# Two tiles go through a layer in lockstep with two output banks each, weights of both layers of a pair are decoded together, and three convolutions run on PE at the start

## The chip, the cores and the metric

The kernel runs on one core of a Trainium2 chip. The metric is device time in microseconds, the median of several executions. The core has PE (TensorE, matrix products), DVE (VectorE), ACT (ScalarE), POOL (GpSimd) and SP (SyncE, which issues most DMAs). Each engine works its own queue in order, and engines wait for each other by semaphores.

## The reference

A causal convolution over the sequence, then two feed-forward layers. There are 16384 tokens of 192 numbers; each layer has 2048 hidden units.

```python
w = softmax(weight, axis=-1)                      # 8 heads x 7 taps
out[b, s, h] = sum_k w[h, k] * x[b, s + k - 6, h] # zeros before the start
x = out.reshape(16384, 192)
x = np.maximum(x @ w_in, 0.0) ** 2 @ w_out        # layer 1
h = x @ w_in2
x = np.maximum(0.01 * h, h) @ w_out2              # layer 2
```

The weights of both layers are float64 in HBM.

## The kernel before

**Tiles and products.** The 16384 tokens are cut into 32 tiles of 512. For accuracy each number is split into a high and a low part, and each product is made of three: high x high, low x high, high x low. The 192 rows of an operand are three blocks of 64. PE works as two halves of 64 rows (`halves`), and products come in pairs, one for each half, that run beside each other. `g1` makes two blocks of 128 hidden units (`h`, two PSUM banks): 18 products of 512 columns. `g2` adds them to the tile's output in four PSUM banks, 20 products for two hidden blocks. A step is one `g1` and one `g2` of the step before; a tile of a layer has 8 steps (`NP`), and the order of tiles is: four tiles of layer 1, two of layer 2, then one of each in turn. The program has 64 x 8 x 38 = 19,456 such products, and 56 more in the first steps that only keep PE busy (`keep_warm`).

**Output banks.** Each half of PE sums into banks of its own: `o[n][i]`, n for the first 128 and the last 64 output columns, i for the half. `evac` copies the four banks out (`take`, on ACT and DVE), adds the halves on DVE, lets GpSimd move 64 rows (L457) and adds again (L460).

**Between the products.** ACT makes `g` from `h` (`act`), ACT or DVE squares it in layer 1 (`square`), ACT rounds it to the high part `hi`, and DVE subtracts to get the low part `lo` (L416). The next `g2` needs `hi` and `lo`.

**Weights.** There are 16 pairs of hidden blocks, eight in each layer, numbered p. For each pair, `load_win` and `load_wout` bring 128 x 384 doubles each, and `decode` turns them into a high and a low part by six operations on DVE and two on ACT for each of the two. The first tile of layer 1 needs a new pair in every step, and so does the first tile of layer 2.

**Preparation.** `prep_tile` loads a tile of x, transposes it on DVE and makes the convolution there, 7 operations (taps) for each of two parts; `split_a` and `split_b` write its high part with ACT, `split_a_lo` and `split_b_lo` its low part with DVE, and then a DMA copies blocks from one half's partitions to the other's (`copy_half`, `x<-x`). One of the first tiles' convolutions is made on PE (`conv_pe`, 7 scaled diagonals).

**Order.** Within a step the order on each engine is that of the code. `pieces` adds single operations of preparation (`prep`), of evacuated tiles (`leave`) and of decoding (`dec`), at most so many a step and within a budget of DVE time. DMAs stand in SP's queue in the order of the program, but for a few on ACT's.

Of the kernel before, what the change touches and what calls it, by code (L numbers as in the profile page):

```python
# [20 lines left out]
WB = 3  # L21
STEP = 4100
DEBT = -4000
LEAD_I, LEAD_O = 2, 1
LEAD_X = 2.5
SPACE = 0.8
LEAVE = 5
WARM = 4
# [4 lines left out]
def conv_moe_moe2_kernel(  # L33
# [10 lines left out]

# [7 lines left out]
    NT = B * S // TT  # L61
    R = D - P
    HALO = 32
    HT = HALO + TT

    const = ctx.enter_context(tc.tile_pool(name="const", bufs=1))
    stage = ctx.enter_context(tc.tile_pool(name="stage", bufs=3))
    px = ctx.enter_context(tc.tile_pool(name="px", bufs=XB))
    p1 = ctx.enter_context(tc.tile_pool(name="p1", bufs=1))
    pz = ctx.enter_context(tc.tile_pool(name="pz", bufs=4))  # L70
    pg = ctx.enter_context(tc.tile_pool(name="pg", bufs=4))
    ph = ctx.enter_context(tc.tile_pool(name="ph", bufs=4))
# [3 lines left out]
    f32 = lambda ap: ap.bitcast(F32)  # L76
    halves = lambda i: slice(R * i, R * i + R)

    bias_e = const.tile([P, 1], F32, name="bias_e")
    nc.gpsimd.memset(bias_e, -896.0 * 2.0 ** 23)  # L80

    TURN = ((0, 1), (1, 0), (2, 2))
    W = {}
    for l in (1, 2):
        W[l] = dict(

            i=const.tile([P, NP, 3, 2, P], F32R, name=f"i{l}"),

            o=const.tile([P, NF, 2 * P + 2 * R], F32R, name=f"o{l}"),
        )
    w_in = {1: w_in1.bitcast(I32), 2: w_in2.bitcast(I32)}
    w_out = {1: w_out1.bitcast(I32), 2: w_out2.bitcast(I32)}
    NE = 3 * P

    scal = deque()

    def flush_scal():
        while scal:  # L100
            scal.popleft()()

    def decode(word, shape, outs):

        lo_w, hi_w = word[..., 0], word[..., 1]
        n = shape[1] * shape[2]
        view = lambda t: t[:, 0:n].rearrange("p (c d) -> p c d", d=shape[2])
        T = {}  # L110
        one, two = 70 + n * 52 // 100, 70 + n * 104 // 100

        def exponent():

            T["t"] = view(stage.tile([P, NE], I32, tag="t", name="t"))
            nc.vector.tensor_scalar(  # L116
                out=T["t"], in0=hi_w, scalar1=0x7FFFFE00, scalar2=None, op0=ALU.bitwise_and
            )

        def rebias():  # L120
            nc.scalar.activation(out=T["t"], in_=T["t"], func=ACTF.Relu, scale=8.0, bias=bias_e)

        def mantissa():
            T["m"] = view(stage.tile([P, NE], I32, tag="m", name="m"))
            nc.vector.tensor_scalar(out=T["m"], in0=hi_w, scalar1=0x1FF, scalar2=None, op0=ALU.bitwise_and)  # L125

# [247 lines left out]
    def keep_warm(u, n):  # L374

        if not ready:
            ready.append(a_bank())
# [415 lines left out]
```

## Time and profile before

| | |
|---|---|
| median of 3 runs | 2216.11 us (2214.8 to 2217.06) |
| span of the profiled execution | 2215.3 us |
| PE, DVE, ACT, POOL busy | 97%, 66%, 65%, 4% of the span |
| PE busy in the first of 40 slices | 70% |
| mean granted clock of PE | 0.993 |

The profiled execution's own time is not told apart from its span; the span lies within the times of the three runs. Busy shares of PE overlap, since products are pipelined: how far PE is from its best pace is read from the number of products in a stretch, not from its busy time.

### The profile page before, as it was taken

The numbers are of one execution on the slowest core, as the hardware profiler recorded it, in microseconds if no ns is written. First come the engines' busy times: TensorE is split into PE (matmuls) and PEld (weight loads), VectorE is DVE, ScalarE is ACT, GpSimd is POOL, SyncE is SP. The second block draws the span as 40 slices with busy tenths as digits, with TensorE's granted clock in tenths as the row PEclk, the third lists the DMA queues.
The fourth block names the chain that finished last, engine by engine and source line by source line (L and its number), as shares of the span: only waits on it lengthen the run. The fifth ranks groups of instructions, "written<-read, shape, count | busy, mean of one in ns | idle before, by whom it ended". The sixth has DMA issues, their size and how long they took to land.

```text
span 2215.3 us, 46852 instructions
## 1 busy us (share of the span) xinstructions
PE 2155.8 (97%) x19554; PEld 1810.3 (82%) x19554; DVE 1469.1 (66%) x2345; ACT 1445.9 (65%) x2681; POOL 80.1 (4%) x143
## 2 busy tenths in 40 slices
PE   7988999999999999999999999999999999999998
PEld 3866888888888888888888888888888888888887
DVE  7757855766756676665766666676665767666554
ACT  4868656666666666666666666666666666666664
POOL 0000000000000000000000000000000000000000
PEclk8999999999999999999999999999999999999999
DMA  5223211121212112122221212112121221211111
GB/s 131 75 65 84 43 31 38 35 37 29 44 36 46 37 26 48 25 44 40 39 39 20 44 35 46 37 27 46 26 44 39 41 42 17 47 29 38 37 23 15
DMA packets 227256, 91.09 MB, mean 41 GB/s; under 512 B 204516, under 2 KB 214756, under 8 KB 227044
## 3 DMA queue, kind: packets, MB, share of 16 engines
q1 hardware_dynamic: 224772, 86.74, 20.0%
q8 instruction: 152, 2.49, 0.5%
q10 hardware_dynamic: 2272, 1.38, 0.3%
q14 instruction: 60, 0.49, 0.1%
HBM read 25.17 MB, written 12.58 MB: 17 GB/s over the span
## 4 chain that ended last, share of the span: by engine, by line
PE 85%; ACT 6%; DVE 5%; issue 2%; DMA 1%; SPq 0%; ACTq 0%; POOL 0%; DVEq 0%; POOLq 0%
PE o L362 45%; PE h L362 40%; ACT hi L412 2%; ACT g L399 1%; ACT g L408 1%; DVE lo L416 1%; DVE g L406 1%; DVE t L135 1%; ACT x L349 1%; DVE m L128 1%; DMA w<-in_moe_w_in_dram 0%; DVE t L116 0%; ACT x L337 0%; PE conv L303 0%; DVE m L125 0%
## 5 line engine op out<-in xcount | busy, mean ns | idle before, releaser
L362 PE MATMUL h<-x,i 64*128 64x512 f32 x9272 | 1103.1, 377 | 13.5 <-DVE i L150 7.7
L362 PEld LDWEIGHTS h<-x,i 64*128 64x128 f32 x9272 | 893.4, 187 | 139.2 <-DVE i L150 8.0
L416 DVE TENSOR_TENSOR lo<-g,hi 128x512 fp32r<-128x512 f32 x1024 | 693.2, 695 | 293.7 <-ACT hi L412 275.3
L362 PE MATMUL o<-hi,o 64*128 64x512 f32 x6144 | 873.0, 377 | 3.2 <-ACT hi L412 2.9
L362 PEld LDWEIGHTS o<-hi,o 64*128 64x128 f32 x6144 | 600.3, 186 | 93.5 <-ACT hi L412 5.5
L412 ACT CAST hi<-g 128x512 fp32r<-128x512 f32 x1024 | 605.9, 620 | 96.3 <-DVE g L406 95.4
L362 PE MATMUL o<-lo,o 64*128 64x512 f32 (+1 forms) x4096 | 641.3, 378 | 27.9 <-DVE lo L416 27.4
L401 ACT ACTIVATE g<-h 128x512 f32<-128x512 f32 x512 | 277.8, 594 | 382.2 <-PE h L362 382.2
L362 PEld LDWEIGHTS o<-lo,o 64*128 64x128 f32 (+1 forms) x4096 | 342.4, 159 | 144.9 <-DVE lo L416 52.9
L399 ACT ACTIVATE g<-h 128x512 f32<-128x512 f32 x512 | 301.0, 588 | 230.4 <-PE h L362 230.1
L406 DVE TENSOR_TENSOR g<-g 128x512 f32<-128x512 f32 x224 | 161.0, 719 | 144.5 <-ACT g L399 144.1
L408 ACT ACTIVATE g<-g 128x512 f32<-128x512 f32 x288 | 182.8, 635 | 8.2
L292 DVE SCALAR_TENSOR_TENSOR acc_a<-xT_a,taps,acc_a 128x512 f32<-128x512 f32 x180 | 134.0, 745 | 2.7
L457 POOL COPY z<-z 64x512 f32<-64x512 f32 x64 | 56.0, 875 | 1660.8 <-DVE z L455 1636.2
L455 DVE TENSOR_TENSOR z<-z 128x512 f32<-128x512 f32 x128 | 83.2, 680 | 0.0
L452 DVE COPY z<-o 128x512 f32<-128x512 f32 x128 | 82.0, 682 | 1.0 <-PE o L362 1.0
L340 DVE TENSOR_TENSOR x<-z,x 128x512 fp32r<-128x512 f32 x32 | 22.1, 691 | 87.4 <-ACT x L337 87.4
L340 DVE TENSOR_TENSOR x<-acc_a,x 128x512 fp32r<-128x512 f32 x30 | 21.1, 704 | 81.7 <-ACT x L337 81.7
L292 DVE SCALAR_TENSOR_TENSOR acc_b<-xT_b,taps,acc_b 128x512 f32<-128x512 f32 x96 | 71.9, 749 | 1.8
L452 ACT COPY z<-o 128x512 f32<-128x512 f32 x128 | 69.0, 596 | 1.8 <-PE o L362 1.8
L353 DVE TENSOR_TENSOR x<-z,x 64x512 fp32r<-64x512 f32 x32 | 21.8, 683 | 71.0 <-ACT x L349 71.0
L460 DVE TENSOR_TENSOR z<-z 64x512 f32<-64x512 f32 x64 | 43.2, 676 | 2.3 <-POOL z L457 2.3
(67 smaller groups left out, 399.9 us busy)
## 6 DMA issues: line engine op xcount, KB each, us to landing
x<-x SPq DMA_DIRECT2D x189, 256.0 KB
raw_a<-in_x_dram SPq DMA_DIRECT2D x128, 64.0 KB
out_dram<-y_a SPq DMA_DIRECT2D x126, 64.0 KB
w<-in_moe_w_out_dram SPq DMA_DIRECT2D x16, 384.0 KB
raw_b<-in_x_dram SPq DMA_DIRECT2D x64, 64.0 KB
out_dram<-y_b SPq DMA_DIRECT2D x63, 64.0 KB
w<-in_moe_w_in_dram SPq DMA_DIRECT2D x15, 192.0 KB
w<-in_moe_w_in_dram SPq DMA_DIRECT2D x45, 64.0 KB
```

The costliest lines, as they stand in the source:

```text
L292: nc.vector.scalar_tensor_tensor(out=acc[0], in0=src, scalar=w, in1=acc[0], op0=ALU.mult, op1=ALU.add)
L340: nc.vector.tensor_sub(out=operand_view(X[u][:, 0, 1, :]), in0=taken(u, src), in1=operand_view(f32(X[u][:, 0, 0, :])))
L362: nc.tensor.matmul(out=o.rearrange("p (b a) -> p b a", a=2), lhsT=w, rhs=z.rearrange("p (a b) -> p b a", a=2), start=begin, stop=end_,)
L399: nc.scalar.activation(out=g, in_=hps.pop((u, f)), func=ACTF.Relu)
L401: nc.scalar.activation(out=g, in_=hps.pop((u, f)), func=ACTF.Prelu, alpha=0.01)
L406: nc.vector.tensor_mul(out=g, in0=g, in1=g)
L408: nc.scalar.activation(out=g, in_=g, func=ACTF.Square)
L412: nc.scalar.copy(out=a, in_=gsp[u, f])
L416: nc.vector.tensor_sub(out=b, in0=gsp.pop((u, f)), in1=f32(hi[u, f]))
L452: (nc.vector.tensor_copy if i else nc.scalar.copy)(out=z[n, i], in_=o[n][i])
L455: nc.vector.tensor_add(out=z[n, 0], in0=z[n, 0], in1=z[n, 1])
L457: nc.gpsimd.tensor_copy(out=z[1, 1][0:R], in_=z[1, 0][R:2 * R])
```

## The change

**Lockstep.** A phase now is a layer for two tiles (`u = (l, q)`, tiles 2q and 2q + 1). A step is one `g1` of one of them, pair p for tile i, so that a weight pair serves two steps. 512 steps of 18 + 20 products. `g2(u, f)` adds one hidden block f of both tiles, two steps after the `g1` (`LAG`). The order is two phases of layer 1, two of layer 2, and so on.

**Banks.** Each tile has two banks, `m` for 128 columns and `r` for 64. In a first part of `g2`, half 0 of PE writes tile 0's bank `m` and half 1 tile 1's; in a second part they change over. An instruction of GpSimd waits for the last product of the first part, and the first product of the second part waits for GpSimd. Two groups of `g1` (`AHEAD`, two pairs) stand between the parts. In the next step the second part's assignment is kept for the first.

**Evacuation.** Per two tiles: ACT and DVE copy one bank `m` each, ACT copies 64 rows of each bank `r`, and DVE adds 64 rows of each. Nothing of it is on GpSimd, and the small halo copies of the convolution move from GpSimd to DVE.

**Decoding.** The input and output weights of a pair are decoded as 768 columns, except the first pair (two parts of 384). The last three operations are made in two pieces of 640 and 128 columns, since the results lie in two tensors.

**Start.** The convolutions of the first two tiles, three of 7 taps, are on PE; 14 diagonals are made, 10 of them on DVE and 4 on ACT. Part of x is issued from ACT's queue. Weights are loaded up to three pairs ahead in two buffers and in the space of one later tile. The 56 products of `keep_warm` are gone.

The core of the diff:

```diff
+    def decode(l, p, t, a, b):
+
+        lo_w, hi_w = t[:, a:b, 0], t[:, a:b, 1]
+        n = b - a
+        one, two = 160 + n * 52 // 100, 170 + n * 104 // 100
+        e = min(b, NM)
+        parts = [(lambda z: z[:, 0:e - a], W[l][:, p, 0, a:e], W[l][:, p, 1, a:e])]
+        if b == NW:
+            r = WR[l][:, p]
+            parts.append((lambda z: z[:, NM - a:n].rearrange("p (c d) -> p c d", d=R), r[:, :, 0:R], r[:, :, R:2 * R]))
...
-    def g2(u, p):
-        if p == 0:
...
-        for f in (2 * p, 2 * p + 1):
-            a, b = hi.pop((u, f)), lo.pop((u, f))
-            first, last = f == 0, f == NF - 1
-
-            seq = [(o1, m, a), (o1, ml, a), (o2, r, a), (o2, rh, b), (o1, m, b)]
...
-            for n, (o, c, z) in enumerate(seq):
-                begin = first and id(o) not in begun
...
-                for i in range(2):
-                    v = halves(i)
-                    product(o[i][0:rows], w[v, f, c], z[v], begin, end_)
...
+    def g2(u, f):
...
+        l, q = u
+        if f == 0:
+            ops[u] = {(i, n): ps_o.tile([P, TT], F32, tag=f"o{i}{n}", name=f"o{i}{n}") for i in range(2) for n in "mr"}
+        o = ops[u]
+        a = [hi.pop(((l, 2 * q + i), f)) for i in range(2)]
+        b = [lo.pop(((l, 2 * q + i), f)) for i in range(2)]
+        main = [("m", "m", a), ("m", "ml", a), ("m", "m", b)]
+        rest = [("r", "r", a), ("r", "rh", b)]
+        if f == NF - 1:
+            rest = rest[::-1]
+        for part in range(2):
+            side = part ^ (f % 2)
+            for j, (n, c, z) in enumerate(main + rest):
+                begin = f == 0 and part == 0 and j in (0, 3)
+                end_ = f == NF - 1 and part == 1 and j in (2, 4)
+                for half in range(2):
+                    i = (side ^ half) if n == "m" else 1 - (side ^ half)
+                    v = halves(half)
+                    rows = R if c == "rh" else P
+                    ins = product(o[i, n][0:rows], weights_out(l, v, f, c), z[i][v], begin, end_).ins
+                    if part == 0 and j == 4 and half == 1:
+                        done = nc.gpsimd.nop(nofuse=True).ins
+                        tc.add_manual_dep(done, ins.name, in_turn, reason="halves take turns on a bank")
+                    if part == 1 and j == 0 and half == 0:
+                        tc.add_manual_dep(ins, done.name, in_turn, reason="halves take turns on a bank")
+            yield
...
-        def take(n, i):
-            z[n, i] = pz.tile([P, HT], F32, tag="z", name="z")[:, 0:TT]
-            (nc.vector.tensor_copy if i else nc.scalar.copy)(out=z[n, i], in_=o[n][i])
-
-        def add(n):
-            nc.vector.tensor_add(out=z[n, 0], in0=z[n, 0], in1=z[n, 1])
-            if n == 1:
-                nc.gpsimd.tensor_copy(out=z[1, 1][0:R], in_=z[1, 0][R:2 * R])
-
-        def add_r():
-            nc.vector.tensor_add(out=z[1, 0][0:R], in0=z[1, 0][0:R], in1=z[1, 1][0:R])
-
-        now = [lambda n=n, i=i: take(n, i) for n in range(2) for i in range(2)]
-        adds = [(690, lambda: add(1)), (690, lambda: add(0)), (690, add_r)]
...
+        def take(i):
+            z[i] = new(i)
+            (nc.vector.tensor_copy if i else nc.scalar.copy)(out=z[i], in_=o[i, "m"])
+
+        def shift(i):
+            if i == 0:
+                z["s"], z["r"] = f32(stage.tile([P, NW], I32, tag="m", name="zs")[:, 0:TT]), new("r")
+            nc.scalar.copy(out=z["s"][halves(i)], in_=o[i, "r"][halves(1 - i)])
+
+        def add(i):
+            v = halves(i)
+            nc.vector.tensor_add(out=z["r"][v], in0=o[i, "r"][v], in1=z["s"][v])
+
+        now = [(0, lambda: take(0)), (690, lambda: take(1))]
+        for i in range(2):
+            now += [(0, lambda i=i: shift(i)), (690, lambda i=i: add(i))]
...
-    for s, z in enumerate(steps):
-        first_use.setdefault(("w", z[0][0], z[1]), s)
-        first_use.setdefault(z[0], s)
-
-
-    todo = []
-    for l in (1, 2):
-        for p in range(NP):
-            s = first_use["w", l, p]
-            todo += [(s - LEAD_I, load_win, l, p), (s + 1 - LEAD_O, load_wout, l, p)]
...
-        load_taps()
+        nc.vector.memset(warm_e, 0.0)
+        nc.scalar.activation(out=warm_e, in_=warm_e, func=ACTF.Exp)
+        nc.sync.dma_start(out=w_taps, in_=weight)
...
+        nc.gpsimd.memset(idle, 0.0)
+        make_heads()
+        load_x("b", 0, nc.scalar)
+        load(0)
...
         make_taps()
-        keep_warm_early(3)
-        refill()
-        decode_ahead(1000)
+        keep_warm_early(2)
+        load(1)
+        load(2)
         transpose("a", 0)
         acc0 = conv_pe(xT["a"])
-        decode_ahead(1400)
         transpose("b", 0)
-        accb, pieces = conv("b", 0)
+        for k in range(K):
+            spread_v(1, k)
+        accb = conv_pe(xT["b"], 1)
+        decode_ahead(9)
+        transpose_second()
+        acc1 = conv_pe(second)
         split_a((1, 0), acc0)
...
+        decode_ahead(2)
+        split_a_lo((1, 0), acc0)
+        load(3)
+        decode_ahead(8)
+        split_b((1, 0), accb)
+        split_b((1, 1), accb)
+        decode_ahead(3)
+        split_b_lo((1, 0), accb)
+        split_b_lo((1, 1), accb)
+        decode_ahead(8)
+        split_a((1, 1), acc1)
+        split_a_lo((1, 1), acc1)
+        load_x("b", 2)
+        load_x("a", 2)
...
+        prep_next = 1
+        late = []
+        going = begin_g1(0)
+        for s in range(NS):
+            u, p, i = steps[s]
+            l, q = u
+            t = (l, 2 * q + i)
+            j = 2 * p + i
+            run(going)
+            follows = begin_g1(s + 1) if s + 1 < NS else None
+            leaving = []
+            if s >= LAG:
+                u2, p2, i2 = steps[s - LAG]
+                f = 2 * p2 + i2
+                if s == NS - 2:
+                    run(follows)
+                elif f == 0:
+                    run(follows, GAP)
+                z = g2(u2, f)
+                run(z, 1)
+                if follows:
+                    run(follows, AHEAD)
+                run(z)
+                if f == NF - 1:
+                    leaving, then = evac(u2)
```

**PE, a steady step.** Before, within the second hidden block of one step and the first of the next; `o_1534` and `o_1535` are the two halves' banks of one output, and names in brackets are the semaphores waited for.

```order
L362 MATMUL o_1536<-hi,o_85 128x512
L362 MATMUL o_1537<-hi,o_85 128x512
L362 MATMUL o_1536<-lo,o_85 64x512 [waits DVE_49]
L362 MATMUL o_1537<-lo,o_85 64x512
L362 MATMUL o_1534<-lo,o_85 128x512
L362 MATMUL o_1535<-lo,o_85 128x512
L362 MATMUL o_1534<-hi,o_85 128x512 [waits Activation_49]
L362 MATMUL o_1535<-hi,o_85 128x512
```

Now, from the end of a first part to the beginning of the second; `o0m` and `o0r` are tile 0's banks, `o1m` and `o1r` tile 1's.

```order
L356 MATMUL o0r<-hi,wr_90 128x512
L356 MATMUL o1r<-hi,wr_90 128x512
L356 MATMUL o0r<-lo,wr_90 64x512
L356 MATMUL o1r<-lo,wr_90 64x512
L356 MATMUL h<-x,w_88 128x512 [waits PE_49,Activation_49]
L356 MATMUL h<-x,w_88 128x512 [waits Activation_49]
L356 MATMUL h<-x,w_88 128x512 x2
L356 MATMUL o0m<-hi,w_88 128x512 [waits Pool_sequencer_49]
L356 MATMUL o1m<-hi,w_88 128x512
```

Four products of `g1` have moved between the two parts, and the second part's first product waits for GpSimd's sequencer.

**DVE while weights are decoded.** Before, between two steps' `lo` in the first tile (`t` and `m` are scratch, `w` the loaded doubles).

```order
L416 TENSOR_TENSOR lo<-g,hi 128x512 x2
L116 TENSOR_SCALAR t<-w 128x384
L125 TENSOR_SCALAR m<-w 128x384
L128 SCALAR_TENSOR_TENSOR m<-w,m 128x384
L135 SCALAR_TENSOR_TENSOR t<-w,t 128x384
L145 TENSOR_SCALAR t<-t 128x384
L150 SCALAR_TENSOR_TENSOR o_85<-m,t 128x2x128
L150 SCALAR_TENSOR_TENSOR o_85<-m,t 128x2x64
L116 TENSOR_SCALAR t<-w 128x384
L125 TENSOR_SCALAR m<-w 128x384
L128 SCALAR_TENSOR_TENSOR m<-w,m 128x384
L135 SCALAR_TENSOR_TENSOR t<-w,t 128x384
```

Now, in one of the first 16 steps.

```order
L401 TENSOR_TENSOR lo<-g,hi 128x512 x2
L141 TENSOR_SCALAR t<-w 128x768
L132 TENSOR_SCALAR m<-wide 128x768
L135 SCALAR_TENSOR_TENSOR wide<-wide,m 128x768
L286 SCALAR_TENSOR_TENSOR acc_b<-xT_b,taps,acc_b 128x512 x2
L401 TENSOR_TENSOR lo<-g,hi 128x512 x2
L145 SCALAR_TENSOR_TENSOR t<-w,t 128x640
L145 SCALAR_TENSOR_TENSOR t<-w,t 128x128
L151 TENSOR_SCALAR t<-t 128x640
L151 TENSOR_SCALAR t<-t 128x128
L156 SCALAR_TENSOR_TENSOR w_88<-w,t 128x640
L156 SCALAR_TENSOR_TENSOR wr_90<-w,t 128x2x64
```

Between two steps' `lo` stands half of a pair's decoding with taps of the next tiles' convolution, where both halves of a pair stood.

## Rows read from the trace of the kernel before

**Rows 1.** span and mean granted clock of the core
```profile
core 0: 2215.3 us, clock 0.993
```

**Rows 2.** timeline, a steady step: start, length (us), engine, line, operation, names
```profile
999.76 2.11 PE L362 MATMUL h<-x,i 64*128 64x512 f32 x18
...
1001.90 0.60 ACT L399 ACTIVATE g<-h 128x512 f32<-128x512 f32 x1 [0.98 <-PE h L362]
...
1003.86 2.11 PE L362 MATMUL h<-x,i 64*128 64x512 f32 x18
```

**Rows 3.** L362's products by stretch: busy us (x number), PEclk, DMA share, GB/s
```profile
0.00:60.00 60.00, 21.21 (x150) 17.00 (x151) 0.86 0.51 121
...
60.00:250.00 190.00, 165.57 (x1402) 135.38 (x1401) 0.97 0.27 70
...
250.00:2205.00 1955.00, 1944.56 (x17948) 1647.42 (x17946) 1.00 0.19 36
...
2205.00:2215.40 10.40, 2.15 (x20) 1.43 (x18) 0.74 0.25 38
```

**Rows 4.** waits of weight loads, 60 to 250: us, times, longest
```profile
PEld o L362 <- DVE lo L416: 25.9, 29, 3.1
```

**Rows 5.** timeline, PE after a wait near 117 us
```profile
118.57 3.31 PE L362 MATMUL h<-x,i 64*128 64x512 f32 x18
```

**Rows 6.** groups by line and shape: busy us, mean ns, idle before
```profile
L362 PEld LDWEIGHTS h<-x,i 64*128 64x128 f32 x9272 | 893.4, 187 | 139.2 <-DVE i L150 8.0 <-DMA x<-x 3.6 <-ACT x L349 2.1
...
L416 DVE TENSOR_TENSOR lo<-g,hi 128x512 fp32r<-128x512 f32 x1024 | 693.2, 695 | 293.7 <-ACT hi L412 275.3
...
L399 ACT ACTIVATE g<-h 128x512 f32<-128x512 f32 x512 | 301.0, 588 | 230.4 <-PE h L362 230.1
...
L408 ACT ACTIVATE g<-g 128x512 f32<-128x512 f32 x288 | 182.8, 635 | 8.2
...
L292 DVE SCALAR_TENSOR_TENSOR acc_a<-xT_a,taps,acc_a 128x512 f32<-128x512 f32 x180 | 134.0, 745 | 2.7
...
L128 DVE SCALAR_TENSOR_TENSOR m<-w,m 128x384 f32<-128x384 uint32 x32 | 19.9, 621 | 1.0
...
L121 ACT ACTIVATE t<-t,bias_e 128x384 int32<-128x384 int32 x32 | 19.7, 616 | 14.5 <-DVE t L116 13.1 <-DVE m L125 1.3
...
L150 DVE SCALAR_TENSOR_TENSOR i<-m,t 128x384 fp32r<-128x384 f32 x16 | 8.9, 558 | 0.5
...
L150 DVE SCALAR_TENSOR_TENSOR o<-m,t 128x128 fp32r<-128x128 f32 x16 | 4.5, 284 | 0.0
```

**Rows 7.** timeline, the start: a load, its use, a convolution
```profile
7.83 1.87 SPq L172 DMA_DIRECT2D w<-in_moe_w_in_dram  x3
...
9.18 3.60 PE L303 MATMUL conv<-xT_a,spare_acc_a 128*128 128x512 f32 x8
...
11.43 0.36 DVE L116 TENSOR_SCALAR t<-w 128x384 int32<-128x384 int32 x1 [2.79 <-DMA w<-in_moe_w_in_dram]
```

**Rows 8.** timeline and line L457: hand-overs from engine to engine
```profile
33.22 0.68 DVE L416 TENSOR_TENSOR lo<-g,hi 128x512 fp32r<-128x512 f32 x1
...
33.96 0.48 PE L362 MATMUL o<-lo,o 64*128 64x512 f32 x2 [1.38 <-DVE lo L416]
...
34.28 0.38 PE L362 MATMUL o<-hi,o 64*128 64x512 f32 x2
...
42.36 0.70 DVE L276 STREAM_TRANSPOSE xT_second<-raw_a 128x512 f32<-128x512 f32 x1
...
43.19 0.19 POOL L277 COPY xT_a<-xT_second 128x6 f32<-128x6 f32 x1 [28.86 <-DVE xT_second L276]
...
L457 POOLq EVENT_SEMAPHORE  x64: 17/17/43, 114.1 to 2210.0; - x64
```

**Rows 9.** timeline, the end: last products, last store
```profile
2206.77 0.38 PE L362 MATMUL o<-hi,o 64*128 64x512 f32 x2
...
2212.21 0.32 SPq L483 DMA_DIRECT2D out_dram<-y_b  x1
```

More of the change, by code (lines that the diff above doesn't have):

```diff
@@ L93, in conv_moe_moe2_kernel @@
[L93 to L109, printed above, removed]
-        T = {}
[L111 to L121, printed above, removed]
+    warm_e = const.tile([P, 1], F32, name="warm_e")
@@ new lines, in decode, with room, operand @@
+        last = [(c, lambda fn=fn: each(fn)) for c, fn in ((two, sign), (one, power), (two, low_))]
+        return [(one, mantissa), (two, rest)], [(one, exponent)], last
+    X, order, split = {}, [], set()
+    g1_left = {(l, t): NP for l in (1, 2) for t in range(NT)}
+    def room(u):
+        return u in X or len(order) < XB or g1_left[order[len(order) - XB]] == 0
+    def operand(u):
+        if u not in X:
+            assert room(u)
+            X[u] = px.tile([P, 3, 2, TT], F32R, tag="x", name="x")
+            order.append(u)
+        return X[u]
@@ new lines, in conv_moe_moe2_kernel, with load @@
+        loads = [(l, p) for l in (1, 2) for p in range(NP)]
+        words, since = {}, {}
+        SIDE = {2: 0, 3: 1, 5: 0}
+        AFTER = {0: 4, 1: 6, 2: 5, 4: 7, 6: 8}
+        def load(n):
+            if n >= len(loads):
+                return
+            l, p = loads[n]
+            since[n] = now[0]
+            if n in SIDE:
+                t = wide[:, SIDE[n] * 2 * NW:(SIDE[n] + 1) * 2 * NW].rearrange("p (c w) -> p c w", w=2)
+            else:
+                t = stage.tile([P, NW, 2], I32, tag="w", name="w", bufs=2)
+            load_w(l, p, t)
+            words[n] = t
@@ L554, in decode_one @@
+        budget = [0]
         def decode_one():
[L555 removed]
+            cost, fn = dec.popleft()[1:3]
             fn()
[L557 to L569 removed]
@@ L570, in conv_moe_moe2_kernel, with decode_ahead @@
-        bank = ps_o.tile([P, TT], F32, tag="o11", name="idle_o")
+            budget[0] -= cost
+            return cost
+        def decode_ahead(n):
+            for _ in range(n):
+                decode_one()
+        bank = ps_o.tile([P, TT], F32, tag="o1r", name="idle_o")
         def keep_warm_early(n):
@@ L766 @@
+        high(*late[0])
+        low(*late.pop())
+        while leave:
+            leave.popleft()[2]()
+        for f in range(NF - LAG, NF):
+            run(g2(steps[-1][0], f))
+        at_once, then = evac(steps[-1][0])
+        for c, fn in at_once:
+            fn()
+        for z in then:
+            z[1]()
 _INS = ["x", "weight", "moe_w_in", "moe_w_out", "moe2_w_in", "moe2_w_out"]
```

615 lines of the change are left out of this document (275 added, 340 removed).

## The prediction

> **What bounds the kernel now.** I began with the span [rows 1] and a step of the steady middle, in order of time. There a step of 38 products (19 pairs, one for each half of the array) starts every 1003.86 - 999.76 = 4.10 us [rows 2], 0.2158 us a pair or 0.1079 us a product, with no idle mark on PE. That is the fastest pace in the trace, and the change leaves the number of products at 19,456, so 19,456 x 0.1079 = 2099.3 us is a floor for both kernels. Whatever can be won is what the span has above it: 116 us.
>
> Where these lie shows in the table of stretches, which counts products [rows 3]; a stretch less 0.1079 us for each product is its loss. To 60 us: 94 useful products (150 less the 56 that only keep PE warm, which the reader counts in the code), loss 49.9. From 60 to 250 us: 38.7. From 250 to 2205 us: 18.4. After that: 8.2. So three quarters of the loss lies in the first 250 us, while weights are decoded; the long middle loses under 1%. The waits of 60 to 250 us name the reason: PE's weight loads stood 25.9 us for `lo`, which DVE makes [rows 4]. DVE decodes there, in its one queue, between the `lo`. [...]
>
> **The change part by part.** The sum is made against the profiled execution: span 2215.3 us, with some 0.8 us around it to the median of 2216.1.
>
> *Lockstep and the first 16 steps.* Before, one tile asks for a new weight pair in every step of 4.1 us. A pair costs DVE, from [rows 6] (the operations not listed taken as their likes of the same size): six bit operations of 0.401, four two-input ones of 0.621, then 0.558, 0.284 and, by the line between these two, 0.42 for the 256 columns between, together 6.15 us. With two `lo` of 0.695 that is 7.5 us of DVE in a step of 4.1: PE must wait. After, a pair serves two steps. Joint decoding makes it, by the line through 128 columns at 0.284 and 384 at 0.558 (1.07 ns a column and 0.147 us fixed), about 5.6 us; if nothing were fixed, 6.15 again. So DVE has, for the 16 steps of the first two tiles: 32 `lo`, 22.2; what is then left to decode (four pairs and half of one), 25.4; the preparation of the next two tiles (21 taps of 0.745, three transposes and four subtractions near 0.70), 20.5. Sum 68.1 us. ACT has 32 times an activation, a square and a cast, 0.588 + 0.635 + near 0.59, 58.0 us; its share of decoding, two casts of 768 columns a pair or about 1.8 us, 8.1; four casts of an operand, 2.5. Sum 68.6. PE needs 65.6. So DVE and ACT both run 3 us over, and each in its one queue waits for the other. I take 10 us lost in this phase: 3 of excess and 7 of such waits. Bounds: 3, and the 25.9 of [rows 4].
>
> *The second 16 steps.* DVE: 22.2 of `lo`, 16 squares near 0.70 (11.2), two thirds of eight pairs (29.9), evacuation and operands 4.8: 68.1 against 65.6. I take 3 us (0 to 10). Later phases have less than a step's 4.1 us on either engine.
>
> *The start.* Three convolutions on PE are 42 products of about 0.43 us [rows 7]: 18 us from about 8 us on, so 26 us; before, one was there and DVE did the others. But PE's first steps wait for more. The second tile's copies are issued behind its subtraction, and DVE's queue up to there holds the first three pairs (6.15 for the one in two parts, 2 x 5.6), three operations of the fourth (2.4), seven scaled diagonals of about 0.25, two transposes, four subtractions (2.8): 25.7 us from about 7.9, so 33.6 us if DVE never waits. (The small halo copies that move from GpSimd to DVE, 0.19 each by [rows 8], and the four issues of x that move from SP to ACT are inside these roundings: DVE has to wait for the diagonals, and ACT for the first weights, anyway; without that cover they cost 2 us.) Two copies at about 0.6 us on SP, then 1.7 to land (the load issued by 9.70 was used at 11.43 [rows 7]): 37 us. The first two tiles' first steps, 18 pairs or 3.9 us, are done at about 37.7, loss 33.8. PE stood before that, so I add 3 us at half clock, as in [rows 5]. 37 us. Below, nothing that DVE must do goes away: 31. Above, DVE waits for weights, whose loads stand in SP's one queue with the copies: 47.
>
> Together the decode stage loses 37 + 10 + 3 = 50 us instead of 88.6.
>
> *The token.* Each step of the second layer's products now ends its first part with a hand-over: its last product tells GpSimd, GpSimd tells PE, and the second part's first product waits, with everything behind it in PE's queue. Two pairs of `h` lie between. 512 of them. From the start of that last pair, T: the first reader of a pair started at 1001.90, and that pair at 999.76 + 8 x 0.2158 = 1001.49, so 0.41 [rows 2]. GpSimd's own wait instruction takes 0.017, a copy there began 0.13 after its producer (43.19 against 43.06). From DVE's end at 33.90 to PE's weight load at 33.96 it is 0.06 [rows 8]. So the load may start between T + 0.49 and T + 0.60. It has to start by T + 0.647 - 0.107 = T + 0.54: after a wait the next pair came 0.32 later, 0.107 more than usual, so that much of a load shows. The token is thus between 0.05 early (nothing) and 0.06 late (509 x 0.06 = 31 us). I take nothing, since the instruction is the same as the 0.017 one and no copy follows it. Three tokens at the end have no cover: 3 x (0.49 + 0.107 - 0.216), 1.1 us.
>
> [...]
>
> *Lag and evacuation.* g2 runs two steps behind g1, so `lo` has a whole step more. Before, four half sums are copied and added, three additions a tile and one copy on GpSimd; after, DVE and ACT do three small operations each for two tiles. None of that was on the path except at changes of tile. New is that all four banks are claimed together: from the end of one pair of tiles to the next lie 12 pairs, 2.6 us, plus three main pairs before the shifted bank is written. In layer 1 ACT's queue there is an activation, two casts, a square and an activation (3.0 us) and then three copies near 0.6, and DVE's last addition 0.7: 5.5 us after g1 against 5.6 needed. An operand's cast ahead of them makes it 0.6 late. I take 0.25 for 30 changes, 7.5 us, and 4.5 us for steps in which preparation fills DVE: 12 instead of 18.4. Bounds: 0, and 30 x 0.7 + 9 = 30.
>
> *The end.* Before, from the last products to the last store's issue 5.8 us [rows 9], 8.2 in all. After, one copy, two additions, three transposes on DVE and twelve stores on two queues, about 0.5 us longer, and 1.1 for tokens: 10 (9 to 13).
>
> **Sum.** 2099.3 + 50 + 0 + 12 + 10 = 2171.3, with 0.8 around it 2172, and about 1 for the products at the edges, which the table counts twice: 2173 us, 43 below the median.
>
> **The rivals.** *The decode stage gains half.* DVE and ACT stay the bound and wait for each other as now: 25.9 instead of 10, and 47 for the start: 2173 + 26 = 2199. For it speaks that both are over 100% for 16 steps; against it, that weights are decoded up to three pairs ahead and `lo` has a step of slack. Chance 0.18.
>
> *The banks become the wait.* 30 changes at 0.7 and full preparation steps: 2173 + 18 = 2191. For: ACT's queue order. Against: the second layer's queue has no square. Chance 0.10.
>
> *The token is late, and the kernel slower.* If GpSimd answers like its copies (T + 0.60) and the waiting load must be whole, 0.187 as in the group of weight loads [rows 6], it must start by T + 0.46, is 0.14 late, and 509 x 0.14 = 71 us make 2244. The gain is gone from 43 / 509 = 0.085 us late on. For: PE's queue lets nothing pass a waiting product. Against: the 0.017 row, and the 0.107 that a load cost after a wait. Chance 0.10; in between (0.02 to 0.08 late, 2183 to 2214), 0.06.
>
> That the change doesn't do what it says would mean PE at the old loss to 250 us, 2212: chance 0.03. The forecast has the rest, 0.53.
>
> **How the numbers follow.** The forecast's own range is 2158 to 2190: 6 less at the start, 7 in the first phase, 3 after it; 10 and 7 more. With the other cases in up to 2214, and only the slow token (0.10) and the best of the forecast (0.06) out, 2155 to 2214. A measurement of this kernel can tell about 0.2% (4 us) from no change. Faster holds all but the slow token, what lies over 2212, and half of the 0.03: 0.86. Same 0.04, slower 0.10.
>
> **What would show it.** Right: a step of 4.10 us across a token, with no idle mark on the product behind it; PE at full count from about 40 us, and 300 to 2150 us within 12 us of the floor; about 50 us lost to 250 us; decode groups of 768 columns near 1.1 us for two-input operations. Wrong: a gap before every second part (GpSimd as releaser, some 509 times); PE waiting for `lo` past 100 us in many steps; waits for ACT's copies of `o` once in 16 steps; copies `x<-x` that land after 40 us because SP issues weight loads ahead of them.

## The result and the profile after

The changed kernel takes 2192.07 us (median of four runs, 2190.58 to 2193.05), the kernel before 2216.59 us beside it: a ratio of 0.989, 95% interval 0.9876 to 0.9904. That is 24.5 us faster, where the forecast had 43. 2192 is 19 us above the forecast of 2173 and 2 us above the forecast's own range of 2158 to 2190; it lies inside the wider range with the rivals, 2155 to 2214.

The profiled execution's span and clock, which answer to [rows 1]:

```profile
core 0: 2190.3 us, clock 0.995
```

The page's line of busy times, and its chain of the work that ended last, by engine:

```profile
PE 2150.3 (98%) x19510; PEld 2016.6 (92%) x19510; DVE 1339.2 (61%) x2127; ACT 1417.5 (65%) x2601; POOL 3.4 (0%) x19
...
PE 90%; DVE 5%; ACT 3%; DMA 1%; issue 1%; SPq 1%; DVEq 0%; POOL 0%; POOLq 0%
```

The products of L356 by stretch, which answer to [rows 3] (busy us and number on PE, the same for weight loads, granted clock, DMA share, GB/s); the stretch that [rows 3] ends at 250 us is cut at 120 us, where the first two tiles are through layer 1:

```profile
0.00:60.00 60.00, 24.37 (x180) 20.56 (x182) 0.94 0.68 145
60.00:120.00 60.00, 49.46 (x413) 40.17 (x410) 0.94 0.29 71
120.00:250.00 130.00, 124.49 (x1113) 113.64 (x1115) 1.00 0.23 64
250.00:2150.00 1900.00, 1896.80 (x17503) 1805.92 (x17501) 1.00 0.20 36
2150.00:2190.30 40.30, 28.65 (x256) 24.78 (x252) 0.88 0.17 23
```

A stretch less 0.1079 us for each product is its loss, as in the prediction: 40.6, 15.4, 9.9, 11.4 and 12.7 us. The first three are the decode stage: 65.9 us, where the forecast had 50 and the kernel before 88.6. The last two, some 24 us, were forecast at 22. (The products at the edges, counted in two stretches, are the 1 us that the sum lacks to the span less the floor of 2099.3.) So 16 of the 19 us lie in the decode stage, and most of what follows is about those first 250 us.

The waits of PE's weight loads over the whole span show the same (us in all, times, longest); of 24.9 us for `lo`, 21.9 lie before 250 us, against 25.9 in [rows 4]:

```profile
PEld o1m L356 <- DVE lo L401: 24.9, 25, 5.6
...
PEld o1m L356 <- ACT hi L397: 8.9, 10, 2.1
PEld h L356 <- DMA x<-x: 7.7, 3, 5.2
...
PEld o1m L356 <- POOLq L429: 1.1, 2, 0.6
PEld o0m L356 <- POOLq L429: 1.1, 2, 0.6
```

The last two lines are the token: four waits in all, those at the end that nothing covers.

Three moments of the timeline before 120 us name most of them. Operands: DVE ends the second tile's subtraction at 34.05 us (the forecast said 33.6), SP issues its two copies at once, and PE's weight load that waits for the second of them starts at 40.71 us:

```profile
33.36 0.69 DVE L320 TENSOR_TENSOR x<-conv,x 128x512 fp32r<-128x512 f32 x1 [1.61 <-ACT x L317]
...
34.21 1.15 SPq L302 DMA_DIRECT2D x<-x  x2
...
38.40 0.69 DVE L401 TENSOR_TENSOR lo<-g,hi 128x512 fp32r<-128x512 f32 x1 [4.35 <-ACT hi L397]
...
40.71 5.22 PEld L356 LDWEIGHTS h<-x,w 64*128 64x128 f32 x33 [0.98 <-DMA x<-x]
```

So 6.5 us pass from issue to use, and DVE stands idle for 4.35 us meanwhile. Then, from 55 to 90 us, PE waits once in every 5.2 to 5.7 us for `lo`, each time some 1.5 us:

```profile
59.05 0.18 PEld L356 LDWEIGHTS o1m<-lo,w 64*128 64x128 f32 x1 [1.46 <-DVE lo L401]
...
64.72 0.18 PEld L356 LDWEIGHTS o1m<-lo,w 64*128 64x128 f32 x1 [1.49 <-DVE lo L401]
...
69.91 0.18 PEld L356 LDWEIGHTS o1m<-lo,w 64*128 64x128 f32 x1 [1.23 <-DVE lo L401]
```

At 95.8 us DVE's queue stops for weights. The first operation on the ninth pair (`m<-w`, L132) waits for its load, and the eighth pair's last operations (L145 to L156), an operand, a transpose and two `lo` stand behind it:

```profile
98.28 0.68 DVE L132 TENSOR_SCALAR m<-w 128x768 int32<-128x768 int32 x1 [2.49 <-DMA w<-in_moe_w_out_dram]
98.99 1.23 DVE L135 SCALAR_TENSOR_TENSOR w<-w,m 128x768 f32<-128x768 uint32 x1
100.11 1.04 DVE L145 SCALAR_TENSOR_TENSOR t<-w,t 128x640 int32<-128x640 int32 x2
...
104.65 1.25 DVE L401 TENSOR_TENSOR lo<-g,hi 128x512 fp32r<-128x512 f32 x2
```

### The profile page after: what moved, and what is told of

It reads as the page before. It is cut to its first block, busy times and chain, and to the rows that moved or that the text cites. A ratio compares the mean times of both kernels' runs of the same rounds, so it can differ in the third digit from the quotient of the medians.

```text
span 2190.3 us, 46974 instructions
## 1 busy us (share of the span) xinstructions
PE 2150.3 (98%) x19510; PEld 2016.6 (92%) x19510; DVE 1339.2 (61%) x2127; ACT 1417.5 (65%) x2601; POOL 3.4 (0%) x19
## 4 chain that ended last, share of the span: by engine, by line
PE 90%; DVE 5%; ACT 3%; DMA 1%; issue 1%; SPq 1%; DVEq 0%; POOL 0%; POOLq 0%
PE h L356 42%; PE o1m L356 14%; PE o0m L356 14%; PE o0r L356 10%; PE o1r L356 9%; ACT hi L397 1%; DVE lo L401 1%; DVE acc_a L286 1%; DMA w<-in_moe_w_out_dram 1%; ACT g L393 0%; DVE t L145 0%; ACT g L384 0%; ACT w L148 0%; DVE g L391 0%; PE idle_o L590 0%
## 5 line engine op out<-in xcount | busy, mean ns | idle before, releaser
L356 PE MATMUL h<-x,w 64*128 64x512 f32 x9216 | 1203.3, 377 | 6.8 <-DMA x<-x 6.5
L356 PEld LDWEIGHTS h<-x,w 64*128 64x128 f32 x9216 | 1003.1, 187 | 59.4 <-DMA x<-x 7.7
L356 PE MATMUL o1m<-hi,w 64*128 64x512 f32 x2048 | 610.5, 378 | 5.3 <-ACT hi L397 5.1
L356 PE MATMUL o0m<-hi,w 64*128 64x512 f32 x2048 | 609.4, 377 | 0.2
L356 PE MATMUL o1m<-lo,w 64*128 64x512 f32 x1024 | 388.5, 379 | 14.9 <-DVE lo L401 14.7
L356 PEld LDWEIGHTS o1m<-hi,w 64*128 64x128 f32 x2048 | 360.9, 185 | 30.5 <-ACT hi L397 8.9
L356 PE MATMUL o1r<-hi,wr 64*128 64x512 f32 x1024 | 388.4, 379 | 0.0
L356 PE MATMUL o0r<-hi,wr 64*128 64x512 f32 x1024 | 386.9, 378 | 0.0
L356 PE MATMUL o0m<-lo,w 64*128 64x512 f32 x1024 | 386.5, 377 | 0.0
L356 PE MATMUL o0r<-lo,wr 64*64 64x512 f32 x1024 | 385.3, 376 | 0.0
L356 PE MATMUL o1r<-lo,wr 64*64 64x512 f32 x1024 | 385.3, 376 | 0.0
L356 PEld LDWEIGHTS o0m<-hi,w 64*128 64x128 f32 x2048 | 362.4, 185 | 21.0 <-POOLq L429 1.1
L356 PEld LDWEIGHTS o1m<-lo,w 64*128 64x128 f32 x1024 | 190.7, 186 | 25.4 <-DVE lo L401 24.9
L356 PEld LDWEIGHTS o1r<-hi,wr 64*128 64x128 f32 x1024 | 190.7, 186 | 6.5 <-issue 4.8
L356 PEld LDWEIGHTS o0r<-hi,wr 64*128 64x128 f32 x1024 | 190.8, 186 | 1.6
L356 PEld LDWEIGHTS o0m<-lo,w 64*128 64x128 f32 x1024 | 190.7, 186 | 0.4
```

The lines of the kernel that those rows point to most:

```text
L356: return nc.tensor.matmul(out=o.rearrange("p (b a) -> p b a", a=2), lhsT=w, rhs=z.rearrange("p (a b) -> p b a", a=2), start=begin, stop=end_,)
```

## The experiments

All start from the changed kernel. Losses are worked out as above, for the stretches to 60, 60 to 120 and 120 to 250 us: 40.6, 15.4 and 9.9 in the changed kernel. In e3, e7, e10, e13 and e14 a few lines are added that finish a half decoded pair before an evacuation, since both use one buffer; they are meant to move nothing by themselves, which no run shows alone. The kernel before was timed again beside each group of runs, and its medians there run from 2214.4 to 2216.6 us; so a difference of 2 us between runs of two groups is not clear of noise, and the traces carry the argument.

**The eighth pair ahead of the ninth (e1).**

```diff
-                stage_(j + 1, 0)
-                stage_(j, 2)
+                if parts[j][0] == 7:
+                    stage_(j, 2)
+                    stage_(j + 1, 0)
+                else:
+                    stage_(j + 1, 0)
+                    stage_(j, 2)
                 stage_(j + 1, 1)
```

> The last four operations on the eighth pair of weights are issued ahead of the first operation on the ninth; nothing else moves. Theory A (one operation that waits for its weights holds all of DVE's queue, the eighth pair and the lo behind it too): in the kernel with the whole change DVE stands 2.5 us before that operation at 98 us, and PE then waits 5.1 us for lo; the loss between 100 and 120 us falls from 7.6 to 2 us or less and the time from 2192 to 2186 us (2184 to 2188). Theory B (DVE simply has too much to do in the first 16 steps, and the wait only shows where it comes due): the wait turns up some steps later, 2190 to 2193 us.

2186.97 us (2186.48 to 2188.49), span 2185.3. The stretches of L356 in this run:

```profile
0.00:60.00 60.00, 23.22 (x180) 19.41 (x182) 0.94 0.67 145
60.00:120.00 60.00, 52.88 (x460) 43.83 (x460) 1.00 0.30 75
120.00:250.00 130.00, 125.45 (x1115) 113.72 (x1114) 1.00 0.22 62
```

Losses 40.6, 10.4, 9.7: 5.0 us are gone from the middle one, nothing else moved, and the granted clock there is 1.00 instead of 0.94. Theory A holds, and the wait does not turn up later. In whole times the gain is less sharp: the ratio to the kernel before is 0.9874 (0.9858 to 0.9891), against 0.989 (0.9876 to 0.9904) for the changed kernel, 3.5 us apart and with intervals that overlap.

**Loads behind the copies (e2, e9).** In e2 the loads of three pairs go behind the copies:

```diff
+            if hold[0]:
+                held.append(n)
+                return
...
         load(3)
+        hold[0] = True
         decode_ahead(8)
...
         split_a_lo((1, 1), acc1)
+        hold[0] = False
+        for n in held:
+            load(n)
```

> The loads of the fifth, seventh and sixth pairs of weights are issued behind the six operand copies of the first two tiles instead of ahead of them. Theory A (the start is set by the copies, which stand behind loads on SP and share the DMA engines with them): the second tile's copies, issued at 34.2 us as now, land in about 2.5 us instead of 6.4, its first product comes at about 37.3 instead of 40.7 us, and the time is 3 to 4 us less, 2188 to 2189. Theory B (DVE's work in the first 16 steps is the bound): what PE wins at 40 us it gives back as waits for lo before 120 us, 2191 to 2193 us.

2198.64 us (2198.33 to 2199.52), slower than either theory. The start did come earlier: the load that answers to 40.71 stood at 38.41 us. But the three pairs of weights, 15 issues of SP, now stood ahead of the x of the next tiles, and the transpose of that x stopped DVE's queue. The issue of that x on SP's timeline of this run:

```profile
45.90 2.07 SPq L243 DMA_DIRECT2D raw_b<-in_x_dram  x4
```

And DVE's wait for it, in its waits from 30 to 60 us:

```profile
DVE xT_b L263 <- DMA raw_b<-in_x_dram: 8.3, 1, 8.3
```

x was issued at 35.41 us before this edit. So e2 is no test of theory A; e9 holds back two loads only and puts them behind x:

```diff
-            if hold[0]:
+            if hold[0] and n in (5, 6):
...
         load_x("a", 2)
+        hold[0] = False
+        for n in held:
+            load(n)
```

> As the run with the copies first, but only the loads of the sixth and seventh pairs of weights are issued later, and behind the x of the next tiles, which therefore keep their place. Theory A (the loads ahead of the copies cost the start; in the run before the 8.3 us wait of DVE for x, whose loads my edit had pushed back by 10 us, ate the gain): the second tile's first product at about 38.4 instead of 40.7 us, no wait of DVE for x, and 2 us less, 2189 to 2191 us. Theory B (DVE's work bounds the first 16 steps, whenever they begin): the 2.3 us are given back as waits for lo before 120 us, 2191 to 2193 us.

2192.09 us (2190.24 to 2192.81). Its weight load:

```profile
38.46 5.30 PEld L356 LDWEIGHTS h<-x,w 64*128 64x128 f32 x33 [1.01 <-DMA x<-x]
```

It came 2.25 us earlier than in the changed kernel, and there was no wait for x. Losses 38.2, 15.3, 10.1: in this execution, the fastest of the four, the 2.3 us of the start were kept, the first 16 steps did not take them back, and the span is 1.8 us less. That is theory A's mechanism. The median does not show it: it is that of the changed kernel, so whether a user gains from this edit stays open.

**More decoding at the start (e3).**

```diff
         load_x("a", 2)
+        decode_ahead(5)
```

> Five more decoding operations (the fifth pair's first two, three of the fourth pair), about 3.8 us of DVE, are put behind the second tile's subtraction, where DVE stands idle for 4.35 us from 34.05 us. Theory A (DVE's queue bounds the first 16 steps, and idle time at the start is what it lacks later): PE waits 3 to 4 us less for lo between 55 and 120 us, 2188 to 2189 us. Theory B (ACT, or the weights' arrival, is the bound there): no change, 2191 to 2193 us. If an operation waits for its weights there, lo comes later: up to 2195.

2189.39 us (2188.24 to 2190.71). Losses 39.1, 13.5, 9.2: work put into DVE's idle 4 us came back as 3.8 us of span in the profiled execution, the fastest of the four; the median is 2.7 us less. PE's waits for `lo` from 40 to 130 us are 12.4 us against 15.6 in the changed kernel. That is theory A's direction and, in the profile, its size; in the median it is less.

**Which engine? Squares out, taps out (e5, e6).**

```diff
-                square(*A, False)
+                if s >= 16:
+                    square(*A, False)
...
-                square(*Z, vector)
+                if s >= 16:
+                    square(*Z, vector)
```

> The squares of the first 16 steps (32 of them, 0.63 us each, on ACT) are left out, so the first two tiles' values are not the reference's; nothing of DVE changes. If ACT's work, or DVE's waits for it, is the bound between 45 and 95 us, the waits of 1.3 to 1.5 us for lo in each step go, and some 10 us: 2180 us (2176 to 2185). If DVE's own work is the bound there, the steps stay at 5.3 us and the time within 3 us of 2192.

2191.71 us (one run). Losses 39.1, 15.3, 10.7: 20 us of ACT's work out of these 16 steps changed the time by no more than one run can tell. The taps of the next tiles instead, on DVE:

```diff
+            if q == 1:
+                skip = b_taps[1:] + a_taps[1:] + z_taps[1:]
+                all_ = [z for z in all_ if not any(z[1] is t[1] for t in skip)]
```

> 18 of the 21 taps of the third and fourth tiles' convolution are left out, so these tiles' values are not the reference's: 18 x 0.75 = 13.5 us less for DVE in the first 16 steps, nothing less for ACT. If DVE's work is the bound there, the waits for lo between 45 and 95 us go, and 8 to 12 us: 2182 us (2179 to 2185). If ACT or the hand-overs between the two are the bound, 2189 to 2193 us.

2186.65 us (one run). Losses 38.4, 10.8, 10.7; 5.4 us of span for 13.5 us of DVE's work. PE's waits from 40 to 130 us in this run, where the changed kernel has 15.6 for `lo` and 0.2 for `hi`:

```profile
PEld o1m L356 <- DVE lo L401: 5.0, 6, 3.1
PEld o1m L356 <- ACT hi L397: 4.7, 4, 2.3
```

But the stop for the ninth pair is gone in this run too. The pair's load was issued at 85.72 us, and DVE's operation on it starts without a wait:

```profile
93.44 0.59 DVE L132 TENSOR_SCALAR m<-w 128x768 int32<-128x768 int32 x1
```

e1, which takes out that stop alone, leaves 10.4 in the middle stretch, and this run 10.8. So the 4.6 us gained there are no more than the stop, and 13.5 us of DVE's work less are not seen to gain anything beside it. No theory of a single busy engine fits: once DVE has room, PE waits for `hi` of ACT, which is busy for only 75.5 of these 90 us.

**Joint decoding undone (e7).**

```diff
-            parts = [(0, 0, NI), (0, NI, NW)] + [(n, 0, NW) for n in range(1, len(loads))]
+            parts = [(n, a, b) for n in range(len(loads)) for a, b in ((0, NI), (NI, NW))]
```

> Joint decoding alone is undone: every pair of weights is decoded in two parts (384 and 384 columns) as the first one is, which by the forecast's rows costs DVE 0.55 us a pair, and some 0.25 us more for the four operations of 128 columns that are split off. Theory A (DVE's queue bounds the decode stage): seven pairs in the first 16 steps and eight later cost 5 to 9 us more to 250 us: 2197 to 2201 us. Theory B (waits between DVE and ACT, or loads, are the bound; smaller pieces even let lo through earlier): 2189 to 2194 us.

2223.43 us (2221.86 to 2224.74), ratio to the kernel before 1.0033 (1.0021 to 1.0046): with this one part undone the whole change is a loss. Losses 45.9, 28.0, 14.1, and 20.4 instead of 11.4 from 250 to 2150 us, since decoding now ends at 278 instead of 237 us. Both theories were far off, and the busy engines do not explain it: from 40 to 250 us DVE is busy for 153.1 us and ACT for 143.4, less than in the changed kernel (160.4 and 155.3). DVE's waits from 40 to 250 us in this run:

```profile
DVE t L151 <- ACT w L148: 31.6, 22, 5.5
```

One of them on DVE's timeline:

```profile
53.82 0.36 DVE L151 TENSOR_SCALAR t<-t 128x384 int32<-128x384 int32 x1 [4.20 <-ACT w L148]
```

And what ACT did meanwhile, on its timeline:

```profile
52.27 0.60 ACT L384 ACTIVATE g<-h 128x512 f32<-128x512 f32 x1 [2.68 <-PE h L356]
52.76 0.61 ACT L397 CAST hi<-g 128x512 fp32r<-128x512 f32 x1
53.28 0.51 ACT L148 CAST w<-t 128x384 fp32r<-128x384 f32 x1
```

DVE needs ACT's cast of a weight (L148) before it may clear its bits (L151). The cast stands in ACT's queue behind an activation that waits for PE. PE in its turn stands longest for `hi`, as soon after this moment:

```profile
60.51 0.18 PEld L356 LDWEIGHTS o1m<-hi,w 64*128 64x128 f32 x1 [4.23 <-ACT hi L397]
```

That `hi` stood in ACT's queue behind its share of the weights, which waited for DVE. From 40 to 250 us PE's weight loads waited 22.1 us for `hi`, against 3.1 in the changed kernel, and DVE waited 31.6 us in 22 times for the cast, against 7.0 in 11: twice as many hand-overs, and each of them longer. The granted clock from 60 to 120 us was 0.80, against 0.94, so a part of the 28.0 is clock. That these hand-overs make up the 31 us is argued from the waits. A rival was not tried: within a step the program adds at most two operations of preparation and decoding in layer 1 (`MANY`) unless one is due, and in two parts a pair has twice as many of them.

**The token with one pair of cover (e4).**

```diff
-AHEAD = 2
+AHEAD = 1
```

> One pair of products instead of two covers the hand-over through GpSimd. Where nothing covers it, at the end of the kernel with the whole change, ten pairs and a hand-over take 2.54 us instead of 2.16, so it costs 0.38 us bare. Theory A (that latency is there each time and two pairs just hide it): with one pair 0.38 - 0.216 = 0.16 us show at each of some 508 hand-overs, 83 us: 2275 us (2260 to 2290). Theory B (the latency shows only at the end, since elsewhere GpSimd has answered before): no change, 2190 to 2194 us. If the short stops lower the granted clock, much more than 2300 us.

2263.8 us (2262.99 to 2264.64). The waits of PE's weight loads over the whole span of this run:

```profile
PEld o1m L356 <- POOLq L429: 76.5, 256, 0.6
PEld o0m L356 <- POOLq L429: 76.4, 255, 0.6
```

And the long middle by the stretches of L356:

```profile
250.00:2150.00 1900.00, 1899.10 (x16868) 1513.47 (x16866) 1.00 0.20 36
```

Now 511 hand-overs show. The middle loses 79.9 us instead of 11.4, in 16868 / 38 = 444 steps: 0.154 us each, against 0.16 expected. Theory A. The whole kernel lost 72 us more and not 83, since to 250 us, where PE waits for other things anyway, it lost no more than the changed kernel (64.4 against 65.9). The granted clock stayed at 1.00 through these short stops.

**One convolution back on DVE (e12).**

```diff
-        for k in range(K):
-            spread_v(1, k)
-        accb = conv_pe(xT["b"], 1)
+        ab, b_taps = conv("b", 0)
+        for c, fn in b_taps:
+            fn()
+        accb = ab[0]
```

> One of the three convolutions goes back from PE to DVE: seven taps (5.0 us) instead of seven scaled diagonals (1.5 us) in DVE's queue ahead of the decoding of the first pair. PE has 14 products less there. Theory A (DVE's queue up to the second tile's subtraction sets the start): everything behind comes 3.5 us later, 2195 to 2197 us. Theory B (the copies' landing, or PE's convolutions, set it, or a later bound catches the delay): 2191 to 2193 us.

2196.27 us (2194.3 to 2198.02). The second tile's copies are issued at 37.84 us, 3.6 later, and PE's load stands at 44.90: theory A. Losses 42.6, 17.5, 11.3. The profiled execution was the slowest of the four, 6 us of span longer; the median is 4.2 us more, close to the delay.

**The second 16 steps (e14).**

```diff
-SECOND, THIRD = 16, 40
+SECOND, THIRD = 16, 34
...
-            vector = l == 1 and s >= 2 * NP
+            vector = l == 1 and s >= 4 * NP
```

> In the second 16 steps all squares stay on ACT (16 of 0.69 us less for DVE), and the second layer's weights are due by step 34 instead of 40, so that more of them is decoded before the second layer begins. Theory A (what is left to decode after step 32 stands in DVE's queue ahead of lo and makes the 8.8 us lost between 180 and 240 us): that loss falls to 3 to 5 us, 2187 to 2189 us. Theory B (ACT has no room in the second 16 steps): the loss from 120 to 180 us rises from 1.2 by 3 us or more, 2190 to 2196 us. Theory C (the weights' loads, two buffers, set the pace): no change, 2191 to 2193 us.

2189.58 us (2187.99 to 2192.53), but the profiled span is 2190.8. Losses 41.9, 16.6, 7.4: the last stretch is 2.5 better, the first two 2.5 worse, although nothing there was changed. No verdict from this.

**Together (e10, e13).** e10 has the edits of e1, e3 and e9; e13 those of e1, e3 and e14.

> The order of the eighth and ninth pairs, the five operations more at the start, and the late loads of the sixth and seventh pairs, all three. If the three causes are independent their spans' gains add up, 5.0 + 3.8 + 2.0: 2181 us (2179 to 2183). If they are one and the same shortage of DVE, the largest of them is all: 2186 to 2187 us.

2186.01 us (2185.53 to 2186.63), losses 38.7, 8.5, 12.8. The gains do not add up: the time is 1 us less than e1's. In this execution 120 to 250 us is worse by 3; e13, without the late loads, does not show that.

> Three edits together: the eighth pair's last operations ahead of the ninth pair's first, five more operations at the start, and the squares of the second 16 steps on ACT with the second layer's weights due by step 34. Theory A (they remove waits in three stretches, 100 to 105 us, 34 to 60 us and 180 to 240 us; the first two were seen to add up to little, 2186.0 for both with the late loads): 2187.0 - 2.5 for the second 16 steps - 1 for the start = 2183.5 us (2181 to 2185.5). Theory B (what one wins the next takes back, as between the first two): 2186 to 2188 us.

2184.23 us (2182.41 to 2185.03), ratio to the kernel before 0.9857 (0.984 to 0.9873). That is the forecast of theory A, but not by its places, as the stretches of L356 show:

```profile
0.00:60.00 60.00, 24.36 (x188) 21.02 (x190) 0.94 0.67 145
60.00:120.00 60.00, 54.19 (x478) 46.05 (x476) 1.00 0.29 75
120.00:250.00 130.00, 124.38 (x1112) 110.64 (x1110) 1.00 0.22 62
```

Losses 39.7, 8.4, 10.0: against e1 the gain lies before 120 us, and the last stretch is as it was. It is the fastest version here, 8 us below the changed kernel; that it beats e1 rests on medians 2.7 us apart, whose intervals to the kernel before overlap.

## Why the prediction was right in sign and 19 us off

The parts of the sum follow one by one. The lower end of the forecast's own range should read 2157 (2173 less 6, 7 and 3), not 2158; nothing rests on it.

**The floor and the middle: right.** The steady pace is unchanged, and 250 to 2150 us lost 11.4 us where 12 were forecast for lag and evacuation. The same 11.4 or 11.5 stood in ten other runs (all but e4 and e7), so it is a property of the order there. The sum is right, and both of its terms are there, but in other sizes. These waits stand in the list of the whole span:

```profile
ACT x L317 <- DVE acc_a L286: 23.6, 8, 3.1
PEld o1r L356 <- issue: 4.8, 15, 0.4
```

From 250 to 2150 us PE's load for bank `o1r` waits 14 times for some 0.33 us, 4.6 us in all, just behind DVE's addition of that bank (L455); the forecast had 30 changes of 0.25, 7.5. And in seven steps PE waits for a `hi` and then a `lo`; that is most of the other 6.8 us, where the forecast had 4.5 for steps in which preparation fills DVE. In each of the seven a cast of an operand (L317) stands in ACT's queue for 3.1 us, until DVE has made the last tap, and the step's activation and `hi` stand behind it. No run moved that cast.

**The token at nothing: right, and by a small margin.** PE's products across one hand-over in the steady middle of the changed kernel, on its timeline (no idle mark on the one behind it):

```profile
1000.27 0.38 PE L356 MATMUL o0r<-lo,wr 64*64 64x512 f32 x1
1000.31 0.38 PE L356 MATMUL o1r<-lo,wr 64*64 64x512 f32 x1
1000.49 0.62 PE L356 MATMUL h<-x,w 64*128 64x512 f32 x4
1000.92 0.38 PE L356 MATMUL o0m<-hi,w 64*128 64x512 f32 x1
```

The weight loads of the same moment:

```profile
1000.28 0.43 PEld L356 LDWEIGHTS h<-x,w 64*128 64x128 f32 x4
1000.79 0.18 PEld L356 LDWEIGHTS o0m<-hi,w 64*128 64x128 f32 x1
```

The waiting load starts 0.48 us after T (1000.31, the later product of the pair): the working said 0.49 to 0.60, and that it must start by 0.54. It does so 0.06 early, and the product follows on the grid, 1000.92 - 1000.49 = 2 x 0.2158. With one pair less of cover the limit is 0.324, so the load is 0.156 late, and e4 measured 0.154. Put the other way, e4 alone gives the margin: two pairs cover the hand-over with 0.2158 - 0.154 = 0.06 us to spare. The rival of the slow token falls.

**The start, 37: 3.6 short.** The step that failed is "then 1.7 to land". DVE's part came out to half a microsecond (34.05 against 33.6); the copies took 5.3 us from the end of their issue to PE's load. SP was issuing the load of the sixth pair right ahead of them, and the 16 DMA engines moved 230 GB/s from 30 to 40 us. The 1.7 had been read from a quieter moment: 108 GB/s were moved from 9.70 to 11.43 us in the kernel before. e9 took 2.25 us of it away. In e2, e9 and e10, where loads are moved behind the copies, PE's load stands 4.4 to 4.5 us behind the copies' issue, in the five runs with unmoved loads listed at the end of this document 6.5 to 7.5. So the loads ahead of the copies were the larger part of the 3.6; the rest stays open. The prediction had named such copies after 40 us as a sign of being wrong, and they came. The half clock of the 3 us in the 37 is what the traces show: 0.50 was granted from 118 to 121 us in the kernel before, in the 18 products of [rows 5], and 0.50 from 42 to 44 us in the changed kernel, behind the wait for the copies. What it cost the start was not measured apart.

**The first 16 steps, 10: 5.4 short.** The 10 came out as a sum: without the stop for the ninth pair e1 loses 10.4 from 60 to 120 us. Its parts, 3 of excess and 7 of waits between the queues, are not shown: with 13.5 us less for DVE (e6) no excess of DVE is left, and 10.8 are lost all the same; with 20 us less for ACT (e5) the loss is that of the changed kernel. So the waits remain, and that the sum fits is in part luck. What failed is that the step saw the weights' arrival as a danger for the start alone. In fill_dec the next pair's first operation is queued ahead of the last ones of the pair in hand; when its load, issued at 90.03 us, right behind the operation that frees its buffer (L156, to 90.00), is not there, all of DVE waits. That is 5.0 us, shown by e1. PE's full count, forecast from about 40 us on, came at 120 us.

**The second 16 steps, 3: enough; the third 16, nothing: 8 short.** 9.9 us were lost from 120 to 250 us. The second 16 steps are 608 products, and from 120 to 187 us 609 were made: 1.3 us lost, less than the 3. From 187 to 250 us it was 507 products and 8.3 us. The step that failed is "Later phases have less than a step's 4.1 us on either engine": a third of the second layer's weights is decoded behind step 32, and PE waits there again for `lo` (5.5 us) and `hi` (2.9). Moving that work earlier (e14) improved the stretch in one profile and not in another (e13), so its cause is not settled.

**Joint decoding: right in work, far too small in worth.** A pair costs DVE 5.8 us by the groups after, against 5.6 forecast. (The 0.401 of its bit operations stands in none of its rows; it is the mean of L116 in the trace before, where L145 took 0.355, so a pair took 6.05 rather than 6.15.) The forecast gave 0.55 us of work a pair, some 8 us in all; undoing it costs 31. By the waits in e7 what joint decoding saves is mostly hand-overs between DVE's and ACT's queues, and the sum had no term for these but the "7 of such waits".

**The end, 10: 2.7 short.** The hand-overs without cover cost 0.38 us each, four of them, 1.5 instead of 1.1. The rest lies behind the last product, most of it in the stores. DVE's first turned block and what follows it, in the changed kernel:

```profile
2181.36 1.30 DVE L472 STREAM_TRANSPOSE y<-z 128x512 f32<-128x512 f32 x2
2182.10 4.46 SPq L477 DMA_DIRECT2D out_dram<-y  x6
2182.10 4.64 ACTq L477 DMA_DIRECT2D out_dram<-y  x6
```

From the start of the last product (2178.72) to the end of the last issue it is 8.0 us, where [rows 9] has 5.8 and the forecast added half a microsecond; from there to the end of the span it is 3.6 us, where the kernel before has 2.8. Six stores on each queue take 0.75 us apiece.

Of the rivals, "the decode stage gains half" comes nearest (2199), but not by its mechanism: it had 47 for the start and 25.9 for the first 16 steps, where 40.6 and 15.4 were measured. "The banks become the wait" falls with the 11.4 us: PE does wait at the banks, but 14 times for 0.33 us and not 30 times for 0.7.

## What to carry to other kernels

Where two engines pass work back and forth in order, count the hand-overs and ask at each what stands ahead of it in the other's queue; the sum of busy times can be met while both stand (e5, e6 and e7 here). An operation that waits for a load should not be queued ahead of finished work that others need (5.0 us in e1). Moving loads out of one wait's way can put them into another's (8.3 us in e2): list all that SP issues behind them.

## What had not been expected of the hardware

- The same decoding operation has two durations. On 768 columns the masking operation (L132) took 0.55 us and the two-input one (L135) 0.98 us near 20 us, but 0.70 and 1.27 us at 48 us, while `lo` takes 0.69 throughout (0.648 to 0.737 over the whole span). Of the 6 us from 16 to 22, PE, DVE and ACT were busy for 6.00, 5.43 and 2.12; of the 4 us from 46 to 50 for 4.00, 3.56 and 3.32. What makes the operations longer was not shown.
- Copies issued in the same order take different times from run to run. In five runs whose instructions are the same up to there (the changed kernel, e1, e4, e5 and e14) PE's load stood 6.5, 6.9, 6.5, 6.6 and 7.5 us behind the issue of the second tile's copies. The first stretch's loss in them ran from 39.1 to 41.9 us, largest with the 7.5 but otherwise not in the same order; that is as much as some of the effects looked for there.
- A stop of some 0.15 us in every step (e4) left the granted clock at 1.00 in the long middle, while 0.94 was granted from 60 to 120 us in the changed kernel, with its stop of 5.6 us, 1.00 in e1 without that stop, and 0.80 in e7, where the waits of PE's weight loads for `hi` lasted up to 4.7 us (4.23 us up to 60.51 us, 4.17 us up to 76.83 us).
